# Attention and feed-forward layer with an emitted order: halved first load, two memsets on GpSimd, new weights for the last blocks, another tail

## The chip, the cores and the metric

The kernel runs on one core of one Trainium2 chip. The metric is the time of one execution in device microseconds; a run is timed several times and its median counts. A core has five engines that take their own instructions in order and wait for each other by semaphores: PE (TensorE, matrix multiplications into PSUM), ACT (ScalarE, activations such as exp), DVE (VectorE), POOL (GpSimd) and SP (SyncE, which here only issues DMAs). DMAs are also issued from ACT's and POOL's queues.

## The reference

A layer on x of 2048 rows and 448 columns in bf16. The rows are normalised; attention with 16 heads of 28 columns and a feed-forward part of 1792 columns both start from the normalised rows, and the result is x plus the attention's output times a gate.

```python
def _A_ref(x, wqkv, wo):                      # x: normalised rows, H = 16, Dh = 28
    q, k, v = (x @ wqkv).reshape(B, S, 3, H, Dh).transpose(2, 0, 3, 1, 4)
    scores = jnp.einsum("bhqd,bhkd->bhqk", q, k) * Dh ** -0.5
    p = _softmax(scores, axis=-1)
    o = jnp.einsum("bhqk,bhkd->bhqd", p, v)
    return o.transpose(0, 2, 1, 3).reshape(B, S, D) @ wo
def _B_ref(x, w1, b1, w2, b2):
    return _gelu(x @ w1 + b1) @ w2 + b2
xn = _layernorm(x)
s = _A_ref(xn, A_wqkv, A_wo)
g = _silu(_B_ref(xn, B_w1, B_b1, B_w2, B_b2))
return x + s * g
```

## The kernel before

**Tiling.** The 2048 query rows are four chunks C of 512 (each four row tiles t of 128), the 16 heads four groups G of four heads; head columns are padded from 28 to 32, so that four heads fill 128 partitions. A block is one group with one chunk, 16 blocks in all, the last one (group 3, chunk 3) cut along its queries into pieces of 256, 128 and 128. A score tile is 128 keys by 512 queries of one head, 1024 in all; PE writes it into one of the eight PSUM banks (tile `ring`, matmuls of L1701). ACT takes two banks at once (128x1024) or three (128x1536) through exp (L1755) into bf16 tiles. A part of the score tiles, the late ones, goes another way: DVE reads the bank (L2035) and makes the exponential with integer arithmetic (L2108). PV matmuls (L2283) multiply the probabilities with v; v has an extra column, so that the softmax's denominators come out in the same bank. DVE forms the reciprocal (L2333), multiplies (L2338), and PE applies Wo (the matmul helper, L129). The feed-forward part and the projections fill PE between the scores.

**Order.** No order is written out by hand. The Python program holds every step as a task of an engine, with what it reads and writes and an assumed duration, and `run` (L422) picks the next task of each engine by weights; the instructions are emitted in the order that it picks. The table `BP` has one row of weights for each block, and `NQ` the number of late groups of four score tiles that a block is to have. Weights change the order of instructions only. A task with priority `HOT` goes first, and while `K.hot` holds a time for an engine, no other task that would still run at that time is started on it.

**Start.** `loads` (L936) issues the loads: SP takes row tile 0 and row tile 1 of the first chunk of x, ACT's queue tiles 2 and 3 (L945), two slices of the q and k weights (L952) and the first tile of chunk 1 (L955). DVE computes the statistics of tiles 0, 1 (L1017), ACT those of tile 3 (L1040, L1046); L1053 and L1055 make the reciprocal standard deviation, L1072 (DVE) and L1076 (POOL) the normalised rows, which PE transposes. The value weights `wv` are 128x4x452 with four padding columns, and rows 64 to 127 of the fourth part are padding as well; `late_pads` sets the padding to zero on DVE (L860 to L862), `vpads` sets the extra columns of v on POOL (L925, L926).

**Tail.** The last piece of the last block is 128 queries. `p_den` (L2186) copies what is there of the denominators with DVE (L2195), spreads it with a selector matmul into a bank `K.den`, and adds the last score tiles' sums with matmuls of ones (`t_ones`, L2228). `p_epi4` copies the piece's PV bank to `E_sb` with ACT (L2312), `p_norm4` takes the reciprocal of the bank and multiplies. `p_out` and `p_last` apply Wo to the row tile (c, t), and `t_oev` (L2392) brings the result to memory: by default DVE multiplies the bank with the gate (L2404); where `PATH` names the tile and no exps are left, ACT copies the bank (L2400) and DVE multiplies the copy (L2402). For chunk 3 and half of chunk 2, DVE then adds x (L2410) and SP issues the output DMA (L2414); for the others, a DMA of POOL adds to x in memory. L1672 on DVE makes the last gate, that of tile (3, 3).

Of the kernel before, what the change touches and what calls it, by code (L numbers as in the profile page):

```python
# [7 lines left out]
ACTF = mybir.ActivationFunctionType  # L8
ALU = mybir.AluOpType
# [5 lines left out]
D = 448  # L15
# [3 lines left out]
G = 4  # L19
C = 4  # L20
# [31 lines left out]
)  # L52
NQ = (14, 4, 4, 4, 7, 14, 7, 16, 8, 15, 5, 9, 6, 9, 12, 8)
# [51 lines left out]
EA = 1  # L105
# [4 lines left out]
PATH = {(1, 2): 'D', (1, 3): 'D', (2, 0): 'D', (2, 1): 'D', (2, 2): 'D', (2, 3): 'D', (3, 2): 'D', (3, 3): 'D'}  # L110
XADD = ()
# [37 lines left out]
class _Kernel:  # L149
# [127 lines left out]

    def dma(self, E, fn, dsem, reads=(), writes=(), land=None):
# [140 lines left out]
    def run(self):  # L419
        idle = 0  # L420
        while True:
            self.settle()  # L422
            if self.next_m >= MTOT and all(p[3].prio >= 90 if isinstance(p[3], _Task) else p[3][0] == "bank" and self.lq_end and not self.lq for p in self.procs):
                return
# [276 lines left out]
    def schedule(self):  # L701
# [48 lines left out]
        K.n_mg = 0  # L750
        K.blk = 0
# [81 lines left out]
    def constants(self):  # L833
# [22 lines left out]
        def late_pads():  # L856
            yield ("until", lambda: K.b_xnT[0][1].tw is not None)

            def f(eng):
                eng.memset(K.wv[64:128, 3, :], 0.0)  # L860
# [62 lines left out]
        def vpads():  # L923
            yield ("until", lambda: K.b_wsq[0].tw is not None)
            yield _Task(POOL, lambda eng: eng.memset(K.vaug[:, :, :, DH:DH + 1], 2.0), K.b_xn[0], [K.b_vpad0], 1.2, 0.05, VPP)  # L925
            yield _Task(POOL, lambda eng: eng.memset(K.vaug[:, :, :, DH + 1:32], 0.0), [K.b_vpad0], [K.b_vpad], 1.2, 0.05, VPP)  # L926
# [9 lines left out]
    def loads(self):  # L936
# [6 lines left out]
        ld(K.x_sb[:, 0, 0, :], xr[0][:, 0, :], K.s_x0t, [K.b_x0t], 3.2)  # L943
# [1242 lines left out]
    def p_den(self, q, ms):  # L2186
# [9 lines left out]
        K.den = yield ("bank", lambda: K.ready([K.b_E[0]]), 1)  # L2196
        den, td = K.den
        yield _Task(PE, lambda eng: _mm(eng, den[:, 0:128], K.selb[:, :], Ea, True, False), [K.b_E[0], K.b_selb], [td], 0.1, 0.12, 1)
# [19 lines left out]
    def t_ones(self, p):  # L2218
        K = self
        den, td = K.den  # L2220
        fl, rd = [], []
        for m in p:
            ap, tk = K.p_slot(m)
            _, j, pc, _, _ = K.pieces(m)
            rd.append(tk)
            for i, (t, q0, nq, col) in enumerate(pc):
                def f(eng, j=j, q0=q0, nq=nq, col=col, ap=ap, z=(m == MTOT - 1 and i == len(pc) - 1)):
                    return eng.matmul(den[32 * j:32 * j + 32, q0 - 384:q0 - 384 + nq], K.one32[:, :],  # L2228
                                      ap[:, col:col + nq] if len(ap.shape) == 2 else ap[:, col // 128:(col + nq) // 128, :], tile_position=(0, 32 * j), start=False,
                                      stop=z, skip_group_check=True)  # L2230
                fl.append(f)
# [6 lines left out]
        return _Task(PE, fall, rd + [K.b_one32], [td], 0.0155 * len(fl), 0.17, HOT, mode="col")  # L2238
# [67 lines left out]
    def p_epi4(self, s, bank):  # L2306
# [4 lines left out]
        if s == 2 and EA:  # L2311
            yield _Task(ACT, lambda eng: eng.activation(K.E_sb[:, 1, sl], bank[0][:, sl], ACTF.Copy), [bank[1]],  # L2312
                        [K.b_E4[t] for t in ts] + [K.b_E[1]], 0.3, 0.0, 0)
        else:
            yield _Task(DVE, lambda eng: eng.tensor_copy(K.E_sb[:, 1, sl], bank[0][:, sl]), [bank[1]],
                        [K.b_E4[t] for t in ts] + [K.b_E[1]], 0.16 + 0.13 * len(ts), 0.0, 0)
# [5 lines left out]
    def p_norm4(self, t):  # L2322
# [3 lines left out]
        if t == 3:  # L2326
            bank, tok = K.den
        else:
            bank, tok = yield ("bank", lambda: K.g_done[C - 1] and K.ready([tE]), 3)
            yield _Task(PE, lambda eng: _mm(eng, bank[:, 0:128], K.selb[:, :], E, True, True),  # L2330
                        [tE, K.b_selb], [tok], 0.1, 0.12, 3)
        R = K.rf[:, t % 2, :]
        yield _Task(DVE, lambda eng: eng.reciprocal(R, bank[:, 0:128]), [tok], [K.b_rf[t % 2]], 0.96, 0.0, HOT if t == 3 else 1)  # L2333
        if t == 3:
            K.hot = {DVE: K.tE[DVE]}
# [3 lines left out]
                    [K.b_on4[t]], 0.3, 0.0, HOT if t == 3 else 1)  # L2339
        if t == 3:  # L2340
            K.hot = {PE: K.b_on4[3].tw + SEM}
            K.hot[DVE] = K.hot[PE] + 0.43
        K.on4[t] = True

# [47 lines left out]
    def t_oev(self, ps, tok, c, t):  # L2392
# [5 lines left out]
        way = PATH.get((c, t)) if K.exp_u == len(K.units) - 1 and K.next_m >= MTOT else None  # L2398
        if way:
# [8 lines left out]
        if own:  # L2408
# [29 lines left out]
    def p_last(self, t):  # L2438
# [8 lines left out]
        if t == 3:  # L2447
            K.hot = {DVE: tok.tw + SEM}
# [53 lines left out]
```

## Time and profile before

| | us |
|---|---|
| three runs | 414.64, 414.19, 414.06 |
| median | 414.19 |
| profiled execution | 414.75 |
| its span | 412.2 |
| outside the span | 2.56 |

| engine | busy us | share of the span | instructions |
|---|---|---|---|
| PE | 394.2 | 96% | 6146 |
| ACT | 401.4 | 97% | 411 |
| DVE | 345.1 | 84% | 599 |
| POOL | 194.4 | 47% | 218 |

The granted TensorE clock was 1.0 for the whole execution. The span runs from the first to the last event that the profiler saw. Rows of the timeline give the start, the length, the engine, the line, the operation, output and inputs with their shapes, and a count where like neighbours are drawn together; in square brackets stands the idle time before and what ended it. Rows of groups give the count, then busy time and the mean in ns, then idle time before. Rows of the chain give start, length and the work that the end hung on.

### The profile page before, as it was taken

What the parts mean: (1) busy time and instruction counts of PE and PEld (TensorE: products, weight loads), DVE (VectorE), ACT (ScalarE), POOL (GpSimd) and SP (SyncE); (2) the same over time, 40 slices, a digit from 0 to 9 for tenths busy, and PEclk for the clock granted to TensorE, in tenths of its full rate; (3) what the DMA queues carried; (4) which work ended last, traced back from release to release, by engine and by line L of the source; (5) the groups of instructions that cost most, each with busy time, mean ns of one, the idle gap of its engine ahead of it and who ended that gap; (6) DMA issues with size and microseconds to landing.
All of it is one profiled execution on the core that took longest, in us unless ns stands there. A gap on an engine that the chain in (4) does not pass through costs nothing.

```text
span 412.2 us, 14656 instructions
## 1 busy us (share of the span) xinstructions
PE 394.2 (96%) x6146; PEld 143.4 (35%) x6146; DVE 345.1 (84%) x599; ACT 401.4 (97%) x411; POOL 194.4 (47%) x218
## 2 busy tenths in 40 slices
PE   6999999999999999999989999999999999999995
PEld 4443233333322233232224453332333223333453
DVE  8958798896679888989898127999998999899986
ACT  6999999999999999999999999999999999999995
POOL 7594666659983473155633411155156014553041
PEclk9999999999999999999999999999999999999999
DMA  8801110101001010100430100220000103200073
GB/s 251 293 2 42 4 31 2 28 7 27 21 3 30 2 28 7 33 3 1 110 97 14 28 3 7 53 54 13 20 26 7 29 6 58 72 3 27 24 134 102
DMA packets 18784, 17.54 MB, mean 43 GB/s; under 512 B 8942, under 2 KB 15422, under 8 KB 18687
## 3 DMA queue, kind: packets, MB, share of 16 engines
q1 hardware_dynamic: 16878, 13.67, 11.2%
q0 software_dynamic: 1008, 2.49, 3.6%
q8 instruction: 48, 0.79, 0.8%
q10 hardware_dynamic: 832, 0.46, 0.4%
q14 instruction: 18, 0.14, 0.1%
HBM read 12.54 MB, written 2.88 MB: 37 GB/s over the span
## 4 chain that ended last, share of the span: by engine, by line
PE 66%; ACT 18%; issue 7%; DVE 6%; POOL 1%; DMA 1%; DVEq 0%; ACTq 0%; POOLq 0%
PE ring L129 31%; PE ring L1701 18%; PE ring L2283 15%; ACT P L1755 10%; ACT h L1755 7%; DVE st L1017 1%; ACT xnT L1755 1%; PE ring L1514 1%; DVE x_sb L2035 1%; DMA x_sb<-in_A_x_dram 1%; PE ring L1123 1%; DVE h L2035 0%; PE ring L1090 0%; POOL h L1076 0%; DVE vaug L1476 0%
## 5 line engine op out<-in xcount | busy, mean ns | idle before, releaser
L1755 ACT ACTIVATE P<-ring 128x1024 bf16<-128x1024 f32 (+1 forms) x235 | 248.7, 1164 | 1.4 <-PE ring L2283 0.3
L1701 PE MATMUL ring<-qT,kT 32*128 32x512 bf16 (+2 forms) x1132 | 131.4, 359 | 5.6 <-ACT P L1755 1.9
L1755 ACT ACTIVATE h<-ring 128x1024 bf16<-128x1024 f32 (+1 forms) x79 | 85.6, 1175 | 0.4 <-PE ring L2283 0.3
L1701 PEld LDWEIGHTS ring<-qT,kT 32*128 32x128 bf16 x1132 | 36.4, 91 | 120.5 <-ACT P L1755 60.4
L2035 DVE TENSOR_SCALAR vaug<-ring 128x512 uint16<-128x512 f32 x88 | 58.6, 685 | 6.6 <-PE ring L1701 4.6
L129 PE MATMUL ring<-xnT,w 128*32 128x512 bf16 x864 | 57.6, 381 | 0.4 <-DVE w L2035 0.2
L129 PE MATMUL ring<-w,h 128*32 128x448 bf16 x896 | 55.5, 355 | 0.2 <-DVE x_sb L2035 0.2
L2283 PE MATMUL ring<-P,vaug 128*32 128x512 bf16 (+2 forms) x599 | 53.9, 352 | 0.1
L2378 POOL TENSOR_TENSOR qT<-x_sb,E_sb 128x512 bf16<-128x512 f32 x15 | 17.7, 1182 | 67.0 <-PE ring L2283 29.0
L2367 POOL TENSOR_TENSOR rc<-rs,mone 128x16 f32<-128x16 bf16 x11 | 32.7, 2975 | 29.4 <-DMA rs<-E_sb 27.8
L1755 ACT ACTIVATE xnT<-ring 128x1024 bf16<-128x1024 f32 (+1 forms) x40 | 44.0, 1126 | 0.0
L2035 DVE TENSOR_SCALAR w<-ring 128x512 uint16<-128x512 f32 x52 | 34.7, 686 | 2.7 <-PE ring L1701 2.1
L129 PEld LDWEIGHTS ring<-xnT,w 128*32 128x32 bf16 x864 | 20.5, 96 | 26.1 <-issue 6.3
L129 PEld LDWEIGHTS ring<-w,h 128*32 128x32 bf16 x896 | 17.9, 95 | 22.8 <-issue 14.0
L2035 DVE TENSOR_SCALAR h<-ring 128x512 uint16<-128x512 f32 x32 | 21.3, 685 | 3.8 <-PE ring L1701 3.6
L2283 PE MATMUL ring<-h,vaug 128*32 128x512 bf16 (+1 forms) x209 | 23.9, 379 | 0.5 <-ACT P L1755 0.4
L1416 DVE CAST qT<-ring 128x512 bf16<-128x512 f32 x15 | 10.3, 689 | 15.3 <-PE ring L129 15.0
L2283 PEld LDWEIGHTS ring<-P,vaug 128*32 128x32 bf16 x599 | 16.0, 95 | 14.4 <-issue 7.0
L1528 DVE CAST h<-ring 128x512 bf16<-128x512 f32 x24 | 16.4, 688 | 5.0 <-PE ring L129 4.9
L2035 DVE TENSOR_SCALAR x_sb<-ring 128x512 uint16<-128x512 f32 x28 | 18.5, 683 | 2.5 <-PE ring L1701 1.6
L1422 POOL TENSOR_TENSOR qsq<-qT 128x512 bf16<-128x512 bf16 x12 | 12.5, 1040 | 15.6 <-DVE qT L1416 15.6
L129 PE MATMUL ring<-xnT,wk 128*32 128x512 bf16 x232 | 17.9, 383 | 0.0
(245 smaller groups left out, 639.8 us busy)
## 6 DMA issues: line engine op xcount, KB each, us to landing
x_sb<-recs SPq DMA_DIRECT2D x60, 64.0 KB, 2.0
w<-in_B_w_dram SPq DMA_DIRECT2D x1, 1568.0 KB, 7.5
w<-in_B_w_dram SPq DMA_DIRECT2D x1, 1344.0 KB, 7.9
x_sb<-in_A_x_dram SPq DMA_DIRECT2D x2, 448.0 KB, 5.9
out_dram<-in_A_x_dram SPq DMA_DIRECT2D x2, 448.0 KB, 9.2
out_dram<-h POOLq DMA_DIRECT2D x4, 224.0 KB, 5.9
out_dram<-h SPq DMA_DIRECT2D x8, 112.0 KB, 2.0
xnT<-wq POOLq DMA_DIRECT2D x1, 512.0 KB, 5.0
```

What stands on the lines that cost most here:

```text
L129: ins = eng.matmul(out[q:q + 32, :], w[:, q:q + 32], x, tile_position=(0, q), start=start, stop=stop, skip_group_check=True)
L1017: yield _Task(DVE, lambda eng, i=i, t=t: eng.bn_stats(K.st6[:, i, :], K.x_sb[:, c, t, :]), [K.b_x1t if i == 4 else K.b_x[c] if c else K.b_ ...
L1123: return eng.matmul(bank, w[sl, 3, g * 128:(g + 1) * 128], K.xnT[sl, 3, c * 512:(c + 1) * 512], tile_position=pos, start=False, stop=True, ...
L1416: yield _Task(DVE, lambda eng: eng.tensor_copy(qb, bank), [tok], [qr], 0.7, 0.0, dp)
L1422: yield _Task(POOL, lambda eng: eng.tensor_tensor(qs, qb, qb, ALU.mult), [qr], [tq], 1.1, 0.05, 2, port=True)
L1528: yield _Task(DVE, lambda eng: eng.tensor_copy(dst, bank), [tok], wr, 0.69, 0.0, 2)
L1701: return eng.matmul(dst, K.kT[32 * j:32 * j + 32, g, t * 128:(t + 1) * 128], K.qT[32 * j:32 * j + 32, g, c * 512 + q0:c * 512 + q0 + nq], ...
L1755: return eng.activation(reg[:, i0:i0 + n, :], src, ACTF.Exp, scale=SM_SCALE)
L2035: yield _Task(DVE, lambda eng: eng.tensor_scalar(K.part(u, k).bitcast(dt.uint16), K.like(u, bank), SM_SCALE * LOG2E * 128.0, (127.0 - EXP_ ...
L2283: return eng.matmul(acc[32 * j:32 * j + 32, q0:q0 + nq], w, ap[:, col:col + nq] if len(ap.shape) == 2 else ap[:, col // 128:(col + nq) // ...
L2367: yield _Task(POOL, lambda eng: eng.tensor_tensor(K.rc[:, :], K.rs[:, :], K.mone[:, 0:1].to_broadcast([128, 16]), ALU.pow), [K.b_srs, K.b_ ...
L2378: yield _Task(POOL, lambda eng: eng.tensor_tensor(dst, K.rb, E, ALU.mult), [K.b_rb, tE], [K.b_onT[g][c]], 1.15, 0.05, 1, port=True)
```

## The change

There are four parts.

1. In the table of weights, the rows of blocks 12 to 15 get other values (two of the copies behind them are dropped), and `NQ` asks block 13 for 8 late groups instead of 9.
2. The first row tile of x comes in two halves: rows 0 to 63 from SP, rows 64 to 127 from ACT's queue, ahead of that queue's other loads; both count up the same semaphore.
3. Two of the three memsets of the value weights' padding go from DVE to POOL, ahead of the memsets of v's extra columns and behind the squares of a weight (L1161), each with a wait for the one before; the small one stays on DVE.
4. In the tail, `p_norm3` takes the place of the copy to `E_sb` and of `p_norm4` for the last piece: DVE multiplies the PV bank with the reciprocal directly. The selector matmul into the bank of the denominators gets priority. `PATH` loses (1, 3), (3, 2) and (3, 3) and gains (3, 1). `XADD` gives the addition of x for tile (2, 0) to POOL. For tile (2, 3), listed in `PADD`, PE writes x into a bank by a matmul with the identity and adds the gated result by another, ACT copies the bank, and SP issues the DMA from there. `raw` emits an instruction in place, without the planner's choice.

The diff, cut:

```diff
-NQ = (14, 4, 4, 4, 7, 14, 7, 16, 8, 15, 5, 9, 6, 9, 12, 8)
+NQ = (14, 4, 4, 4, 7, 14, 7, 16, 8, 15, 5, 9, 6, 8, 12, 8)
...
-EA = 1
+HX = 0.1
+PADD = ((2, 3),)
...
-PATH = {(1, 2): 'D', (1, 3): 'D', (2, 0): 'D', (2, 1): 'D', (2, 2): 'D', (2, 3): 'D', (3, 2): 'D', (3, 3): 'D'}
-XADD = ()
+PATH = {(1, 2): 'D', (2, 0): 'D', (2, 1): 'D', (2, 2): 'D', (2, 3): 'D', (3, 1): 'D'}
+XADD = ((2, 0),)
...
         def late_pads():
             yield ("until", lambda: K.b_xnT[0][1].tw is not None)
-            def f(eng):
-                eng.memset(K.wv[64:128, 3, :], 0.0)
-                eng.memset(K.wv[0:64, 3, D:WS], 0.0)
-                return eng.memset(K.wv[:, 0:3, D:WS], 0.0)
-            yield _Task(DVE, f, [], [K.b_wvpad], 0.4, 0.05, 1)
+            yield _Task(DVE, lambda eng: eng.memset(K.wv[0:64, 3, D:WS], 0.0), [], [K.b_wvpad], 0.4, 0.05, 1)
...
         def vpads():
             yield ("until", lambda: K.b_wsq[0].tw is not None)
+            K.wait(POOL, K.b_wsq[0].w)
+            K.raw(POOL, lambda eng: eng.memset(K.wv[64:128, 3, :], 0.0), [K.b_wvpad])
+            K.wait(POOL, K.b_wvpad.w)
+            K.raw(POOL, lambda eng: eng.memset(K.wv[:, 0:3, D:WS], 0.0), [K.b_wvpad])
+            K.wait(POOL, K.b_wvpad.w)
...
-        ld(K.x_sb[:, 0, 0, :], xr[0][:, 0, :], K.s_x0t, [K.b_x0t], 3.2)
+        ld(K.x_sb[0:64, 0, 0, :], xr[0][0:64, 0, :], K.s_x0t, [], 3.2)
+        K.dma(ACT, lambda eng: eng.dma_start(K.x_sb[64:128, 0, 0, :], xr[0][64:128, 0, :]), K.s_x0t, writes=[K.b_x0t], land=3.2)
...
-        if s == 2 and EA:
-            yield _Task(ACT, lambda eng: eng.activation(K.E_sb[:, 1, sl], bank[0][:, sl], ACTF.Copy), [bank[1]], ...)
+        if s == 2:
+            K.E_done = NBLK - 1 + s
+            yield from K.p_norm3(*bank)
+            K.banks.append(bank)
+            return
...
+    def p_norm3(self, acc, ta):
+        (d0, td), = K.den
+        R = K.rf[:, 1, :]
+        yield _Task(DVE, lambda eng: eng.reciprocal(R, d0[:, 0:128]), [td], [K.b_rf[1]], 0.96, 0.0, HOT)
+        K.hot = {DVE: max(K.tE[DVE], ta.tw + SEM)}
+        K.banks += K.den
+        dst = K.qT[:, g, c * 512 + 384:c * 512 + 512]
+        yield _Task(DVE, lambda eng: eng.tensor_tensor(dst, acc[:, 384:512], R, ALU.mult), [ta, K.b_rf[1], K.b_qT[g][c]], [K.b_on4[3]], 0.3, 0.0, HOT)
+        K.hot = {PE: K.b_on4[3].tw + SEM}
+        K.hot[DVE] = K.hot[PE] + 0.43 + HX
+        K.on4[3] = True
...
+        if own and (c, t) in PADD and way:
+            bank, tk = yield ("bank", lambda: True, 1)
+            yield _Task(PE, lambda eng: _mm(eng, bank[:, 0:D], K.ident[:, :], xx, True, False), [K.b_x2[c], K.b_id], [tk], 0.19, 0.17, 1)
         if way:
             yield _Task(ACT, lambda eng: eng.activation(o, ps, ACTF.Copy), [tok], [wr], 0.48, 0.0, 1)
...
+        if own and (c, t) in PADD and way:
+            f = lambda eng: _mm(eng, bank[:, 0:D], K.ident[:, :], o, False, True)
+            yield _Task(PE, f, [K.b_id, wr], [tk], 0.19, 0.17, HOT)
+            yield _Task(ACT, lambda eng: eng.activation(o, bank[:, 0:D], ACTF.Copy), [tk], [wr], 0.48, 0.0, 1)
+            K.outs.append(K.dma(SP, lambda eng: eng.dma_start(ov[:, t, :], o), ...))
```

More of the change, by code (lines that the diff above doesn't have):

```diff
@@ L422, in run @@
             self.settle()
-            if self.next_m >= MTOT and all(p[3].prio >= 90 if isinstance(p[3], _Task) else p[3][0] == "bank" and self.lq_end and not self.lq for p in self.procs):
+            if self.next_m >= MTOT and not self.px and all(p[3].prio >= 90 if isinstance(p[3], _Task) else p[3][0] == "bank" and self.lq_end and not self.lq for p in self.procs):
                 return
@@ L2195, in p_den @@
         yield _Task(DVE, lambda eng: eng.tensor_copy(Ea, acc[:, sl]), [tok], [K.b_E[0]], 0.29, 0.0, 0)
-        K.den = yield ("bank", lambda: K.ready([K.b_E[0]]), 1)
-        den, td = K.den
-        yield _Task(PE, lambda eng: _mm(eng, den[:, 0:128], K.selb[:, :], Ea, True, False), [K.b_E[0], K.b_selb], [td], 0.1, 0.12, 1)
+        K.den = []
+        K.hot = {PE: K.b_E[0].tw + SEM}
+        for c0, c1 in ((0, 128),):
+            x = yield ("bank", lambda: True, HOT)
+            K.den.append(x)
+            yield _Task(PE, lambda eng, d=x[0], c0=c0, c1=c1: _mm(eng, d[:, c0:c1], K.selb[:, :], Ea[:, c0:c1], True, False), [K.b_E[0], K.b_selb], [x[1]], 0.08, 0.12, HOT)
+        K.hot = {}
+        td = K.den[0][1]
         for n0, n1, one in DEN:
@@ L2226, in t_ones, with f @@
             for i, (t, q0, nq, col) in enumerate(pc):
[L2227 to L2230, printed above, removed]
+                def f(eng, j=j, col=col, ap=ap, z=(m == MTOT - 1 and i == len(pc) - 1)):
+                    src = ap[:, col:col + 128] if len(ap.shape) == 2 else ap[:, col // 128, :]
+                    for (d, _), c0, c1 in zip(K.den, cut, cut[1:]):
+                        ins = eng.matmul(d[32 * j:32 * j + 32, c0:c1], K.one32[:, :], src[:, c0:c1], tile_position=(0, 32 * j), start=False,
+                                         stop=z, skip_group_check=True)
+                    return ins
                 fl.append(f)
@@ L2310, in p_epi4 @@
         yield ("until", lambda: K.on_done[NBLK - 3])
-        if s == 2 and EA:
[L2312 to L2316, printed above, removed]
+        if s == 2:
[3 more added lines that the diff above has]
+            return
+        yield _Task(DVE, lambda eng: eng.tensor_copy(K.E_sb[:, 1, sl], bank[0][:, sl]), [bank[1]],
+                    [K.b_E4[t] for t in ts] + [K.b_E[1]], 0.16 + 0.13 * len(ts), 0.0, 0)
         K.E_done = NBLK - 1 + s
@@ L2325, in p_norm4 @@
         E, tE = K.E_sb[:, 1, 128 * t:128 * (t + 1)], K.b_E4[t]
[L2326 to L2331, printed above, removed]
+        bank, tok = yield ("bank", lambda: K.g_done[C - 1] and K.ready([tE]), 3)
+        yield _Task(PE, lambda eng: _mm(eng, bank[:, 0:128], K.selb[:, :], E, True, True),
+                    [tE, K.b_selb], [tok], 0.1, 0.12, 3)
         R = K.rf[:, t % 2, :]
-        yield _Task(DVE, lambda eng: eng.reciprocal(R, bank[:, 0:128]), [tok], [K.b_rf[t % 2]], 0.96, 0.0, HOT if t == 3 else 1)
-        if t == 3:
-            K.hot = {DVE: K.tE[DVE]}
+        yield _Task(DVE, lambda eng: eng.reciprocal(R, bank[:, 0:128]), [tok], [K.b_rf[t % 2]], 0.96, 0.0, 1)
         K.banks.append((bank, tok))
@@ L2447, in p_last @@
         if t == 3:
-            K.hot = {DVE: tok.tw + SEM}
+            K.hot = {DVE: tok.tw + SEM + HX}
         yield from K.t_oev(ps, tok, c, t)
```

27 lines of the change are left out of this document (20 added, 7 removed), and 10 rows, old and new, of the table BP.

## The prediction, made before the changed kernel ran

> **What bounds the kernel now.** I read the page's busy times and its chain first, then the timeline of ACT, then ACT's groups in the stretch that the change reorders.
>
> ```profile
> span 412.2 us, 14656 instructions
> PE 394.2 (96%) x6146; PEld 143.4 (35%) x6146; DVE 345.1 (84%) x599; ACT 401.4 (97%) x411; POOL 194.4 (47%) x218
> PE 66%; ACT 18%; issue 7%; DVE 6%; POOL 1%; DMA 1%; DVEq 0%; ACTq 0%; POOLq 0%
> ```
>
> ACT is busy 97% of the span and PE 96%; the chain that ended last gives PE 66% and ACT 18%. So the two run neck and neck: ACT takes one exp after another, and PE has to lay the next scores down in time. The timeline of ACT tells which of them is late (start, length, line, operation, count):
>
> ```profile
> 12.67 10.32 ACT L1755 ACTIVATE P<-ring 128x1024 bf16<-128x1024 f32 x11
> ...
> 372.02 1.13 ACT L1755 ACTIVATE xnT<-ring 128x1024 bf16<-128x1024 f32 x1
> 372.92 1.56 ACT L1755 ACTIVATE P<-ring 128x1536 bf16<-128x1536 f32 x1
> 374.25 1.15 ACT L1755 ACTIVATE xnT<-ring 128x1024 bf16<-128x1024 f32 x1
> ...
> 385.20 1.07 ACT L1755 ACTIVATE xnT<-ring 128x1024 bf16<-128x1024 f32 x1
> 386.40 4.41 ACT L1755 ACTIVATE P<-ring 128x1536 bf16<-128x1536 f32 x4
> ...
> 397.03 4.78 ACT L1755 ACTIVATE P<-ring 128x1024 bf16<-128x1024 f32 x5
> 401.55 1.18 ACT L1755 ACTIVATE xnT<-ring 128x1024 bf16<-128x1024 f32 x1
> 402.86 1.94 ACT L1755 ACTIVATE P<-ring 128x1024 bf16<-128x1024 f32 x2
> 404.69 1.03 ACT L1755 ACTIVATE xnT<-ring 128x1024 bf16<-128x1024 f32 x1
> ```
>
> The distance from one start to the next is the price of an exp with nothing in the way: (401.55 − 397.03)/5 = 0.904 us for 1024 columns, 374.25 − 372.92 = 1.33 us for 1536. A longer distance is a stall: 386.40 − 385.20 = 1.20, so 0.30 too much; 402.86 − 401.55 = 1.31, so 0.41 too much. From the first exp at 12.67 to the end of the last at 404.69 + 1.03 = 405.72 the time is exps plus such stalls. Three things are therefore left for the change: when the first exps start, the stalls in the stretch that it reorders, and the tail after 405.72.
>
> **Part 1, the start.** Rows of the timelines of DVE, ACT, PE and POOL, and POOL's group for a plain memset:
>
> ```profile
> 3.53 1.36 DVE L1017 BATCH_NORM_STATS2 st<-x_sb 128x6 f32<-128x448 bf16 x2 [0.20 <-DMA x_sb<-in_A_x_dram]
> ...
> 5.82 0.73 DVE L1072 TENSOR_SCALAR h<-x_sb,mv,rstd 128x448 bf16<-128x448 bf16 x2
> ...
> 10.38 0.25 DVE L860 MEMSET wv<- 64x226 uint32 x1
> 10.66 0.47 DVE L1261 TENSOR_SCALAR qT<-ring,colK 128x256 bf16<-128x256 f32 x1
> ```
>
> ```profile
> 0.75 0.39 ACTq L945 DMA_DIRECT2D x_sb<-in_A_x_dram  x1
> 3.76 0.58 ACT L1040 ACTIVATE P<-x_sb 128x448 bf16<-128x448 bf16 x1 [1.75 <-DMA x_sb<-in_A_x_dram]
> ```
>
> ```profile
> 11.08 0.97 PE L129 MATMUL ring<-wv,xnT 128*32 128x112 bf16 x64
> 13.88 0.38 PE L1090 MATMUL ring<-ident,h 128*128 128x128 bf16 x4 [0.51 <-DVE st L1017]
> ```
>
> ```profile
> 8.30 1.23 POOL L925 MEMSET vaug<- 128x256 bf16 x1 [0.59 <-DVE h L1072]
> ...
> 12.87 0.87 POOL L1076 TENSOR_SCALAR h<-x_sb,nm,rstd 128x448 bf16<-128x448 bf16 x1 [0.30 <-ACT rstd L1055]
> ```
>
> ```profile
> L1913 POOL MEMSET qpad<- 128x512 bf16 x1 | 0.5, 515 | 0.0
> ```
>
> *The two halves.* DVE stood 0.20 us before its first statistics, waiting for the first x tile. That is the most the halves can bring: after it DVE's own memsets bind. The other way they can cost: ACT's first load, issued at 0.75, was there when L1040 began at 3.76, later than the 3.53 at which the x tile from SP served DVE; if the half on ACT's queue lands like that load, statistics start at 3.76, +0.23. Half the rows should not take as long as that load, so I take −0.10, bounds −0.20 and +0.23. What is queued behind the new issue on ACT: the remaining loads go one issue (0.39) later, so L1040 would run from at most 4.15 to 4.73. DVE's own statistics last to 3.53 + 1.36 = 4.89, which covers it; without that cover it would be 0.39.
>
> *The memsets.* From DVE goes L860 (10.38 to L1261's start at 10.66: 0.28); the 64x2 one that stays is L861's. DVE's q tiles (L1261) come earlier by up to 0.28 plus what the halves bring. But PE's v block (11.08, 0.97 long) and the first scores stand behind work fed by x, so PE moves only by the halves. On POOL come two memsets: 64x452 at no more than L1913's rate, about 0.46, and the 128x12 one, by the same slope near nothing, with its fixed part about 0.1. POOL stood 0.59 before L925; 0.56 plus two waits on its own semaphores fill that hole and push L925 by about 0.05 (0.6 if L1161 had ended later). POOL's xn tile L1076 at 12.87 decides when the transposes at 13.88 and the scores of the third exp come; it waits 0.30 for rstd, and that hides 0.05. Taken: −0.05, bounds −0.20 and +0.10.
>
> Sum for the start: **−0.15**, bounds −0.40 and +0.30.
>
> The Trainium skill ("DMA: Bandwidth & Descriptors", Rules for kernel authors) speaks against the halves: two transfers to disjoint partition halves serialize on the same DMA engines, so one of 128 partitions should be used. The 3.53 row cannot tell, as no tile is split before; by the rule the halves would bring 0 and the start −0.05 (rival 1). The skill's "SBUF — State Buffer" (Who interferes with whom) has DVE's tensor_scalar and GpSimd block each other for whole instructions; the two L1072 at 5.82 took 0.73 for both while POOL was at work, so I add nothing for the new memsets there; by that rule the start would be up to 0.46 worse.
>
> **Part 2, the last blocks.** PE's order is the same for its first 5213 instructions of 6148; after that (about 364 us) blocks 13 to 15 are reordered. The number of exps does not change: still as many of 1024 and of 1536 columns. ACT's groups from 372.3 to 404.6, shapes apart (the count stands after x):
>
> ```profile
> L1755 ACT ACTIVATE P<-ring 128x1024 bf16<-128x1024 f32 x17 | 17.0, 1087 | 0.2
> L1755 ACT ACTIVATE xnT<-ring 128x1024 bf16<-128x1024 f32 x9 | 10.0, 1110 | 0.0
> L1755 ACT ACTIVATE P<-ring 128x1536 bf16<-128x1536 f32 x6 | 9.2, 1533 | 0.1
> ```
>
> From the start at 372.02 to the one at 404.69, 32.67 us, lie 26 exps of 1024 (23.50) and 6 of 1536 (7.98): 31.48. So **1.19 us of stall is all that reordering can win here**; more than a third is the one of 0.41. What causes it, from the chain (start, length, work of PE):
>
> ```profile
> 400.95 0.94 PE ring L129 x16
> 401.89 0.61 PE ring L2283 x32
> 402.50 0.69 PE ring L1701 x16
> ```
>
> Sixteen matmuls of Wo and 32 of PV, 1.55 us, lay between two groups of scores, where ACT had an exp of 0.904 to chew. In the changed order I summed the same way, with these prices, the PE work between score groups. The single steps that preceded a stall (1.62 ahead of 386.40, then 1.95, then 1.87 over two exps) become 1.46 and 1.41 for one exp, and 1.68, 1.52, 1.62 and 2.06 for two. About 0.7 us of the stall should go; the last step grows (32 PV, 24 Wo and 4 selector matmuls ahead of the last scores) and gives back 0.1 to 0.2, smaller ones another 0.15 to 0.25. Taken: **−0.30**, bounds −1.1 (nearly stall-free) and +0.5 (a new order as poor as the worst such stretch I summed elsewhere in the trace, with some 0.35 more stall, and the last step at its upper price).
>
> **Part 3, the tail.** T is the end of the last exp, 405.72.
>
> ```profile
> 404.10 0.62 DVE L2404 TENSOR_TENSOR h<-ring,h 128x448 bf16<-128x448 f32 x1
> ...
> 406.24 0.96 DVE L2333 RECIPROCAL w<-ring 128x128 f32<-128x128 f32 x1 [0.88 <-PE ring L2228]
> 407.30 0.29 DVE L2338 TENSOR_TENSOR qT<-E_sb,w 128x128 bf16<-128x128 bf16 x1
> 407.51 0.38 DVE L1672 TENSOR_TENSOR h<-h,w 128x448 bf16<-128x448 bf16 x1
> ```
>
> ```profile
> 407.65 0.37 PE L129 MATMUL ring<-wo,qT 128*32 128x448 bf16 x4
> 407.68 0.98 ACT L2400 ACTIVATE h<-ring 128x448 bf16<-128x448 f32 x2 [0.21 <-PE ring L129]
> ...
> 408.54 0.69 DVE L2402 TENSOR_TENSOR h<-h 128x448 bf16<-128x448 bf16 x2
> 408.65 1.71 SPq L2414 DMA_DIRECT2D out_dram<-h  x3
> 409.14 0.69 DVE L2410 TENSOR_TENSOR h<-h 128x448 bf16<-128x448 bf16 x2
> ```
>
> Before: reciprocal at T + 0.52, multiply T + 1.58, Wo's last four at T + 1.93, then ACT's copy (to 408.66), DVE's multiply and add (to 409.83 = T + 4.11), then the last output DMA: SP's three issues end at 408.65 + 1.71 = 410.36, and less one issue of 0.39 (as ACT's at 0.75) the last begins at T + 4.25. After: the last exp is one of 1536 columns, so 16 ones matmuls instead of 8 follow it: reciprocal at T + 0.58, its multiply straight from PSUM at T + 1.64 to 1.93 (ACT's copy to E_sb was not late, so its loss saves nothing), Wo to T + 2.35. ACT's copy, half of 0.98 plus the hand-over, and DVE's L2402 leave the path of (3,3); in their place stands one L2404 from PSUM, 0.62 as at 404.10: T + 2.45 to 3.07; the add to T + 3.49. The other late tile, (2,3), gets PE's identity matmuls (0.37 as the row at 407.65) at T + 2.58, ACT's copy 2.98 to 3.52, its DMA issue at T + 3.55. That issue stands ahead of the last one on SP's queue; with 0.39 for it the last begins at T + 3.94, not 3.52. **−0.31**; bounds −0.45 (SP's hold shorter) and +0.10 (reciprocal held by the DVE's L2404 and add of (3,2), which just fit ahead of it).
>
> **Sum.** −0.15 − 0.30 − 0.31 = −0.76. The profiled execution took 414.75 us (412.2 of span and 2.56 around it), so 414.0 there. The three runs have a median of 414.19, the profiled one being the slowest of four; on the median the forecast is 414.19 − 0.76 = 413.43, **413.4**. Its own range, from the start and the last blocks at half or double: −0.3 to −1.2, 413.0 to 413.9.
>
> **Rivals.**
> *1, nothing at the start and nothing in the blocks (413.9).* Both halves land together with what one transfer did, and the reordered blocks move their stalls instead of losing them; −0.31 remains. For it: the stalls before are only 0.3% of the span. Against: the 0.41 one has a plain cause that the new order lightens. Chance 0.12.
> *2, faster (412.4).* The last blocks come out nearly stall-free (−1.1), the start gives its whole −0.40, the tail −0.3: −1.8. For it: ACT ran such stretches already, 397.03 to 401.55 without a stall. Against: PE is 96% busy, so what leaves one gap enters another. Chance 0.24.
> *3, slower (415.3).* The last exp's 12 score matmuls use the bank that DVE's L2404 of tile (3,1) frees, and DVE reaches that only after a copy (0.29 as the multiply), a reciprocal (0.96), a multiply (0.29) and L2404 itself (0.62): 2.16 us in order. ACT then has one or two exps in hand, 0.90 to 1.81, and the scores add about 0.33: a stall of 2.16 + 0.33 − 1.81 = 0.7 to 2.16 + 0.33 − 0.90 = 1.6. It decides from the point where that reciprocal starts less than 1.9 us before PE wants the bank; I count 0.25 us of slack. At 1.6 with the start nearly as before (−0.2) and the tail's −0.31 it is +1.1, 415.3; at 0.7 the whole is about even. For it: DVE takes its queue in order and is 84% busy. Against: the slack is worked out, not guessed, and the order before met no such stall between 402.86 and 404.69. Chance 0.18, of which 0.13 slower.
>
> **How the numbers follow.** Forecast 0.46, rivals 0.12, 0.24 and 0.18. About 0.2%, 0.83 us, is what a measurement of this kernel can tell from no change, and the forecast lies just inside it: I give 0.25 of its 0.46 to faster, 0.21 to same. Faster 0.25 + 0.24 = 0.49, same 0.21 + 0.12 + 0.05 = 0.38, slower 0.13. The range goes from rival 2's middle, 412.4, to 414.9, which takes in rival 3's small end and leaves out some 0.1 on each side.
>
> **What would show it.** First statistics at 3.35 to 3.45 and the first exps 0.1 to 0.2 earlier; over 0.2 later at 3.76 if ACT's half is late. From 372 to the last exp's start, starts further apart than 0.904 or 1.33 add to about 0.9, the largest just before the last exp; over 1.9 there means rival 3, under 0.3 rival 2. The last output issue at about 3.9 after the last exp's end. It is wrong if stalls appear before 364 us, where the order is the same, or if the tail grows.

## The result, and the profile after

The changed kernel takes 416.25 us (median of 8 runs, 415.58 to 417.91), the one before 414.37 (8 runs, 414.06 to 414.88): a ratio of 1.0049, 95% interval 1.0034 to 1.0064. The forecast was 413.4, at most 414.9. By the medians the change costs 1.9 us. Of its eight runs, three (417.45 to 417.91) had a mean granted TensorE clock of 0.996, and the other five (415.58 to 416.64, median 415.85) one of 0.998 to 1.0. The profiled span grew from 412.2 to 413.9.

The page after, its span, busy times and chain:

```profile
span 413.9 us, 14687 instructions
PE 394.9 (95%) x6157; PEld 143.3 (35%) x6157; DVE 346.0 (84%) x595; ACT 400.6 (97%) x409; POOL 195.9 (47%) x221
PE 62%; ACT 20%; issue 8%; DVE 6%; POOL 2%; DMA 1%; ACTq 0%; DVEq 0%; POOLq 0%
```

Busy times hardly moved (PE 0.7 more, ACT 0.8 less), so most of the 1.7 us of span are waiting. Most of this waiting is there before the first exp. The timeline of ACT and its queue after (the line numbers are those of the changed file: L952 is the new half, L954 the load of tiles 2 and 3, L961 the weight slices, L964 the first tile of chunk 1):

```profile
0.77 0.58 ACTq L952 DMA_DIRECT2D x_sb<-in_A_x_dram  x1
1.39 0.82 ACTq L954 DMA_DIRECT2D x_sb<-in_A_x_dram  x1
2.24 0.97 ACTq L961 DMA_DIRECT2D h<-in_A_wqkv_dram  x2
3.24 0.69 ACTq L964 DMA_DIRECT2D x_sb<-in_A_x_dram  x1
...
7.66 0.39 ACT L1158 ACTIVATE wq<-h 128x224 bf16<-128x224 bf16 x1 [1.30 <-DMA h<-in_A_wqkv_dram]
...
13.91 2.95 ACT L1764 ACTIVATE P<-ring 128x1024 bf16<-128x1024 f32 x3
```

The same of before, two rows that the prediction did not show:

```profile
1.17 0.97 ACTq L952 DMA_DIRECT2D h<-in_A_wqkv_dram  x2
2.17 0.49 ACTq L955 DMA_DIRECT2D x_sb<-in_A_x_dram  x1
```

The first exp starts at 13.91 instead of 12.67, 1.24 later. The last load of ACT's queue is issued at 3.24 instead of 2.17: the new half took 0.58 and made the load behind it take 0.82 instead of 0.39. What that does to DVE (timeline after):

```profile
3.36 1.36 DVE L1026 BATCH_NORM_STATS2 st<-x_sb 128x6 f32<-128x448 bf16 x2
...
8.08 0.63 DVE L1026 BATCH_NORM_STATS2 st<-x_sb 128x6 f32<-128x448 bf16 x1 [1.51 <-DMA x_sb<-in_A_x_dram]
8.62 0.99 DVE L1081 TENSOR_SCALAR h<-x_sb,mv,rstd 128x448 bf16<-128x448 bf16 x2
```

The first statistics do start 0.17 earlier, at 3.36, as forecast; but f4 and f2 below, with the tile in one load, start them at 3.36 and 3.38 too, so the runs do not show that the halves did it. The statistics of chunk 1's first tile wait 1.51 for their data and start at 8.08, and before they started at 6.64 without a wait for a load:

```profile
6.64 0.62 DVE L1017 BATCH_NORM_STATS2 st<-x_sb 128x6 f32<-128x448 bf16 x1
```

The chain that ended last runs through that very load:

```profile
3.24 4.81 DMA x_sb<-in_A_x_dram
8.05 0.02 issue
8.08 0.45 DVE st L1026
```

The loads' issue-to-landing times, ACT's queue, after and then before (median where there are two):

```profile
h<-in_A_wqkv_dram ACTq DMA_DIRECT2D x2, 56.0 KB, 3.8
x_sb<-in_A_x_dram ACTq DMA_DIRECT2D x1, 112.0 KB, 4.8
```

```profile
h<-in_A_wqkv_dram ACTq DMA_DIRECT2D x2, 56.0 KB, 3.0
x_sb<-in_A_x_dram ACTq DMA_DIRECT2D x1, 112.0 KB, 3.6
```

So the tile of chunk 1 is issued 1.07 later and takes another 1.2 to land: about 2.3 later in all, against a cover of about 0.85 that it had before. The later of the two weight slices takes 4.9 to land instead of 3.0, and ACT waits for the weights until 7.66. What else was in flight shows on SP's queue, its 336-KB load of the rest of chunk 1, after and then before:

```profile
3.18 0.59 SPq L948 DMA_DIRECT2D x_sb<-in_A_x_dram  x1
```

```profile
2.91 0.58 SPq L940 DMA_DIRECT2D x_sb<-in_A_x_dram  x1
```

Before, ACT's last load was issued 0.74 ahead of that big one (2.17 against 2.91); after, 0.06 behind it (3.24 against 3.18).

By the twelfth exp the delay is 1.63 instead of 1.24, and it stays at 1.63 up to 378 us. In the last blocks, ACT's timeline after:

```profile
396.01 1.10 ACT L1764 ACTIVATE P<-ring 128x1024 bf16<-128x1024 f32 x1
397.36 1.02 ACT L1764 ACTIVATE xnT<-ring 128x1024 bf16<-128x1024 f32 x1 [0.24 <-PE ring L1710]
398.28 5.65 ACT L1764 ACTIVATE P<-ring 128x1024 bf16<-128x1024 f32 x6
404.31 1.03 ACT L1764 ACTIVATE xnT<-ring 128x1024 bf16<-128x1024 f32 x1 [0.38 <-PE ring L1710]
```

By the prices of 0.904 and 1.33, the 32 exps that start from 373.64 to the last one's start at 406.13 (27 of 1024 columns, 5 of 1536) contain 1.43 of stall, where the 32 of before had 1.19. The largest are 0.44 at 397.36 and 0.49 at 404.31. The second hangs on this piece of the chain:

```profile
401.98 0.55 DVE h L2433
402.52 0.04 issue
402.57 1.38 PE ring L128 x28
403.94 0.33 PE ring L1710 x8
```

A multiply of DVE from PSUM, at the end of a run of reciprocals and multiplies that the chain follows from 397.53, lets PE start 28 Wo matmuls at 402.57, and only behind these come the scores of the exp at 404.31. The tail, DVE and SP:

```profile
408.20 0.96 DVE L2359 RECIPROCAL w<-ring 128x128 f32<-128x128 f32 x1
...
410.08 0.62 DVE L2433 TENSOR_TENSOR h<-ring,h 128x448 bf16<-128x448 f32 x1
410.73 0.39 DVE L2447 TENSOR_TENSOR h<-h 128x448 bf16<-128x448 bf16 x1
```

```profile
411.21 0.33 SPq L2443 DMA_DIRECT2D out_dram<-h  x1
411.58 0.43 SPq L2451 DMA_DIRECT2D out_dram<-h  x1
```

With the last exp's end at 407.59 as T, the last output issue begins at T + 3.99, 0.22 less than in the kernel before (409.93, T + 4.21).

### The profile page after: what moved, and what is told of

The parts are those of the page before. It is cut to its first block, busy times and chain, and to the rows that moved or that the text cites. A ratio compares the mean times of both kernels' runs of the same rounds, so it can differ in the third digit from the quotient of the medians.

```text
span 413.9 us, 14687 instructions
## 1 busy us (share of the span) xinstructions
PE 394.9 (95%) x6157; PEld 143.3 (35%) x6157; DVE 346.0 (84%) x595; ACT 400.6 (97%) x409; POOL 195.9 (47%) x221
## 3 DMA queue, kind: packets, MB, share of 16 engines
q0 software_dynamic: 1008, 2.49, 3.6%
HBM read 12.54 MB, written 2.88 MB: 37 GB/s over the span
## 4 chain that ended last, share of the span: by engine, by line
PE 62%; ACT 20%; issue 8%; DVE 6%; POOL 2%; DMA 1%; ACTq 0%; DVEq 0%; POOLq 0%
PE ring L128 30%; PE ring L1710 16%; PE ring L2299 14%; ACT P L1764 11%; ACT h L1764 7%; ACT xnT L1764 2%; DMA x_sb<-in_A_x_dram 1%; PE ring L1523 1%; DVE x_sb L2044 1%; DVE st L1026 1%; POOL h L1085 1%; PE ring L1132 1%; DVE h L2044 0%; PE ring L1099 0%; DVE w L2347 0%
## 5 line engine op out<-in xcount | busy, mean ns | idle before, releaser
L1710 PEld LDWEIGHTS ring<-qT,kT 32*128 32x128 bf16 x1131 | 35.5, 91 | 120.3 <-ACT P L1764 59.5
L2044 DVE TENSOR_SCALAR vaug<-ring 128x512 uint16<-128x512 f32 x92 | 61.1, 684 | 5.9 <-PE ring L1710 3.8
L1764 ACT ACTIVATE xnT<-ring 128x1024 bf16<-128x1024 f32 (+1 forms) x39 | 43.0, 1130 | 0.6 <-PE ring L1710 0.6
L2299 PE MATMUL ring<-h,vaug 128*32 128x512 bf16 x201 | 23.4, 383 | 0.5 <-ACT P L1764 0.4
L2044 DVE TENSOR_SCALAR h<-ring 128x512 uint16<-128x512 f32 x28 | 18.8, 686 | 3.8 <-PE ring L1710 3.6
```

What stands on the lines that cost most here:

```text
L1710: return eng.matmul(dst, K.kT[32 * j:32 * j + 32, g, t * 128:(t + 1) * 128], K.qT[32 * j:32 * j + 32, g, c * 512 + q0:c * 512 + q0 + nq], ...
L1764: return eng.activation(reg[:, i0:i0 + n, :], src, ACTF.Exp, scale=SM_SCALE)
L2044: yield _Task(DVE, lambda eng: eng.tensor_scalar(K.part(u, k).bitcast(dt.uint16), K.like(u, bank), SM_SCALE * LOG2E * 128.0, (127.0 - EXP_ ...
L2299: return eng.matmul(acc[32 * j:32 * j + 32, q0:q0 + nq], w, ap[:, col:col + nq] if len(ap.shape) == 2 else ap[:, col // 128:(col + nq) // ...
```

## The experiments

Kernels that differ only at the start run the same instructions in the same order on PE, ACT and DVE (the moved memsets and loads apart), so each part can be had alone. The times below are medians; "before" ran on the same chip within each group of four. The first exp's start is from each kernel's profile (12.67 in the profile of before; g2, g3 and g4, which have its start, show 12.76 to 12.88, so 0.2 there tells nothing).

| kernel | us | before | ratio, 95% interval | first exp |
|---|---|---|---|---|
| f1 halves alone | 417.40 | 414.51 | 1.0057 [1.0035, 1.0079] | 14.46 |
| f2 memsets alone | 414.74 | 414.51 | 1.0000 [0.9986, 1.0015] | 12.76 |
| f3 both halves from SP | 416.91 | 414.51 | 1.0050 [1.0033, 1.0067] | 15.07 |
| f4 extra 1-KB load on ACT | 416.83 | 414.51 | 1.0038 [1.0021, 1.0056] | 16.09 |
| g1 halves, SP's big load held | 414.71 | 414.67 | 1.0000 [0.9986, 1.0014] | 12.91 |
| g2 change without its start | 414.61 | 414.67 | 1.0000 [0.9989, 1.0010] | 12.88 |
| g3 new weights alone | 415.08 | 414.67 | 1.0018 [1.0006, 1.0030] | 12.76 |
| g4 new tail alone | 414.56 | 414.67 | 0.9992 [0.9979, 1.0005] | 12.82 |
| h1 change, SP's big load held | 415.33 | 414.96 | 1.0013 [1.0000, 1.0027] | 12.63 |
| h2 change, one slice moved to SP | 415.00 | 414.96 | 1.0004 [0.9989, 1.0019] | 13.15 |
| h3 change, first tile in one load | 415.07 | 414.96 | 1.0011 [0.9996, 1.0025] | 12.67 |
| h4 before, SP's big load earlier | 415.19 | 414.96 | 1.0012 [1.0000, 1.0024] | 13.52 |

**f1, the halves alone.**

```diff
-        ld(K.x_sb[:, 0, 0, :], xr[0][:, 0, :], K.s_x0t, [K.b_x0t], 3.2)
+        ld(K.x_sb[0:64, 0, 0, :], xr[0][0:64, 0, :], K.s_x0t, [], 3.2)
+        K.dma(ACT, lambda eng: eng.dma_start(K.x_sb[64:128, 0, 0, :], xr[0][64:128, 0, :]), K.s_x0t, writes=[K.b_x0t], land=3.2)
```

> The kernel before with one part of the change alone: the first x tile in two halves, one from SP and one from ACT's queue. Theory A (the new issue at the head of ACT's queue makes that queue's other loads late): the first x tile lands at about 3.2 instead of 3.5, tiles 2 and 3 at about 4.6 instead of 3.7, the first tile of chunk 1 at about 8 instead of 5.8; the first exp starts at about 13.9 instead of 12.67, and the time rises by 1.4 to 1.9 us, so nearly all of the measured +1.9. Theory B (the two memsets on GpSimd hold the start up): no change or a gain, 414.0 to 414.5, first exp at 12.5 to 12.7. Theory C (cutting the tile in two is what costs, wherever the halves are issued): as A here.

Measured: +2.9 us by the medians, +0.57% by the comparison (1.5 to 3.3 us, where A had 1.4 to 1.9), first exp at 14.46. The halves alone cost what the whole change costs, and B falls. The timeline of DVE has the same wait, longer:

```profile
8.72 0.63 DVE L1018 BATCH_NORM_STATS2 st<-x_sb 128x6 f32<-128x448 bf16 x1 [2.13 <-DMA x_sb<-in_A_x_dram]
```

**f2, the memsets alone** (the two moved as in the change's diff).

> The kernel before with the two memsets of the value weights' padding moved to GpSimd alone. Theory A: within 0.2 us of before (414.2 to 414.5), first exp at 12.5 to 12.7, the memsets inside GpSimd's hole of 0.59 us ahead of the memsets of v. Theory B: GpSimd's chain comes 0.5 us or more later, the first exps at 13.2 or later and the time at 415 or more.

Measured: no difference beyond the interval of ±0.15%. In its profile the exps fall 0.48 behind by the twelfth, so a few tenths are there; see h3.

**f3, both halves from SP.**

```diff
-        K.dma(ACT, lambda eng: eng.dma_start(K.x_sb[64:128, 0, 0, :], xr[0][64:128, 0, :]), K.s_x0t, writes=[K.b_x0t], land=3.2)
+        ld(K.x_sb[64:128, 0, 0, :], xr[0][64:128, 0, :], K.s_x0t, [K.b_x0t], 3.2)
```

> The kernel before with the first x tile in two halves, both from SP; ACT's queue is left as it was. Theory A: ACT's loads land as before (the first tile of chunk 1 at about 5.8 to 6.1), SP's later loads come 0.4 to 0.6 later; the first exp within 0.4 us of 12.67, the time between 414.2 and 414.9. Theory C: the first exp at about 13.9 and 415.8 to 416.3, as with halves from two queues.

A's number is missed: +0.50%. ACT's loads are as before, but now the first tile itself is late. DVE's first statistics:

```profile
4.91 1.36 DVE L1018 BATCH_NORM_STATS2 st<-x_sb 128x6 f32<-128x448 bf16 x2 [1.58 <-DMA x_sb<-in_A_x_dram]
```

The second half is issued behind the first, at 1.39, and takes 3.5 to land (chain):

```profile
1.39 3.50 DMA x_sb<-in_A_x_dram
```

So DVE starts at 4.91 instead of 3.53, and A is too narrow: it is not ACT's queue that is special. On either queue, what is pushed back is late by more than its issue. SP's 336-KB load is issued only at 3.81 here and not beside the half, so theory D, which the next runs test, does not cover this case. Why the first exp comes 2.40 later when the first statistics come 1.38 later was not followed.

**f4, an extra load of 1 KB on ACT's queue**, with the whole first tile from SP.

```diff
+        K.dma(ACT, lambda eng: eng.dma_start(K.P[0:64, NP - 1, 0:8], xr[0][64:128, 0, 0:8]), K.s_x0b, writes=[], land=3.2)
```

> The kernel before with the whole first tile from SP, and one extra load at the head of ACT's queue that moves only 64 rows of 16 bytes into a spare place that nobody reads. Theory A: the queue's other loads are pushed back as in the change, with nothing gained by an earlier tile: the first exp at 13.5 to 14.1, the time at 415.6 to 416.4. Theory C, or contention by the bytes of the half: within 0.3 us of before.

Measured: +0.38%, and in its profile chunk 1's first tile comes latest of all:

```profile
0.77 0.55 ACTq L944 DMA_DIRECT2D P<-in_A_x_dram  x1
```

```profile
9.04 0.63 DVE L1018 BATCH_NORM_STATS2 st<-x_sb 128x6 f32<-128x448 bf16 x1 [2.42 <-DMA x_sb<-in_A_x_dram]
```

C falls: no tile is cut here, and 1 KB is enough. What costs is one more issue at the head of the queue. But an issue of 0.55 does not explain 2.4: ACT's last load is issued at 2.97 instead of 2.17 and lands some 6.0 after that instead of 3.6. In f1, f4 and the changed kernel its issue falls just beside that of SP's 336-KB load. Theory D says that this company is the price, and g1 and h4 test it from both sides.

The first exp at 16.09, later than A's 13.5 to 14.1, is not the work of the loads alone. In this profile the granted TensorE clock was 0.50 from 12 to 14 us, where it was 1.0 in the kernel before; why it fell is not shown (the window's length, busy time of PE, PEld, DVE, ACT and POOL, then the clock, the DMA share and GB/s):

```profile
12.00:14.00 2.00, 2.00 (x11) 1.45 (x10) 1.64 (x6) 0.95 (x4) 1.94 (x6) 0.50 1.08 309
```

**g1, the halves with SP's big load held back** by two issues of 1 KB.

```diff
+        K.dma(SP, lambda eng: eng.dma_start(K.P[0:64, NP - 1, 448:456], xr[0][64:128, 0, 0:8]), K.s_x[1], writes=[], land=3.2)
+        K.dma(SP, lambda eng: eng.dma_start(K.P[0:64, NP - 1, 456:464], xr[0][64:128, 0, 0:8]), K.s_x[1], writes=[], land=3.2)
         ld(K.x_sb[:, 1, 1:4, :], xr[1][:, 1:4, :], K.s_x[1], [K.b_x[1]], 6.5)
```

> The kernel with the two halves alone, and on SP two extra loads of 1 KB each (64 rows of 16 bytes into a place that nobody reads) right ahead of its 336-KB load of chunk 1's other tiles, so that this load is issued some 1 us later. Theory A, refined to D (what ACT's queue was pushed back by costs most because its last loads then run beside SP's 336-KB load): the last weight slice of ACT's queue lands at about 5.5 to 6 instead of 8, the first tile of chunk 1 at 6 to 7 instead of 8.7; the first exps at 12.8 to 13.8 and the time at least 0.8 us under that of the halves alone (417.4), if the later 336-KB load (about 8.5 to 9) does not take it back. Rival E (each load is late by the issues ahead of it alone, whatever runs beside it): those two land as with the halves alone, and the time is that or up to 1 us more.

Measured: the loss of the halves is gone, 414.71 against 414.67, with more loads, and those of ACT's queue issued later than before. ACT's last load is issued at 3.24 just as in the changed kernel, SP's big one now at 4.46, and the landing time of the former (DMA view) falls from 4.8 to 3.0:

```profile
4.46 0.58 SPq L940 DMA_DIRECT2D x_sb<-in_A_x_dram  x1
```

```profile
x_sb<-in_A_x_dram ACTq DMA_DIRECT2D x1, 112.0 KB, 3.0
```

```profile
6.47 0.62 DVE L1020 BATCH_NORM_STATS2 st<-x_sb 128x6 f32<-128x448 bf16 x1
```

DVE's statistics of chunk 1's tile are back at 6.47, without a wait. E falls. It also shows the most that the halves are worth when nothing is pushed into company: nothing that these runs can tell.

**g2, the change without its start; g3, the new weights alone; g4, the new tail alone** (each the corresponding part of the change's diff).

> The changed kernel with the start of before: one load of the first x tile, memsets on DVE. What is left is the new order of the last blocks and the new tail. Theory A: the first exp at 12.67, the steady part as before, the last exp's start about 0.2 us earlier than before but 0.43 us longer, the tail 0.2 to 0.3 us shorter: 414.0 to 414.6, within 0.1% of before. Rival F (the last blocks hold most of the loss): 415.5 or more.

> The kernel before with the new weights for blocks 12 to 15 and the new number of late groups alone; its tail is that of before. As in the changed kernel some 1.2 to 1.6 us of stall stand between 372 and the last exp: the end of the last exp 0 to 0.4 us later than before and the time 414.3 to 414.9. If the reordering was good and only its match with the new tail bad: 413.5 to 414.1.

> The kernel before with the new tail alone (no copy of the last piece's bank, the direct multiply, x added by PE for one tile, the new paths); weights, late groups and start are those of before. The prediction's tail term of -0.31 says 413.9 to 414.3, the last output's issue at about 3.9 us after the end of the last exp; as measured in the changed kernel, 4.0 us. If the tail saves nothing on its own: 414.4 to 414.7.

Measured: g2 equals before within 0.11%, so the loss is in the start, and F falls. The new weights alone lose 0.18%. The new tail alone wins 0.08%, which its interval does not tell from nothing, though its last output is issued 4.02 after the last exp's end instead of 4.21. In g2 the same two stalls as in the changed kernel, 0.44 and 0.50, are there, 1.43 in all.

**h1, the change with SP's big load held** (g1's two lines), **h2, with one weight slice on SP**, and **h3, with the first tile in one load** (memsets, weights and tail as in the change).

```diff
-        lw(0, 4 * DH, K.s_w["wqk"], K.b_stg, 6.1, (ACT, ACT, SP, SP))
+        lw(0, 4 * DH, K.s_w["wqk"], K.b_stg, 6.1, (ACT, SP, SP, SP))
```

> The changed kernel in full, with the two extra loads of 1 KB on SP ahead of its 336-KB load, nothing else. Theory D (the whole loss is that ACT's pushed-back loads run beside SP's 336-KB load): the last weight slice of ACT's queue and the first tile of chunk 1 land at about 6.0 and 6.2 as in the halves with the same hold, the first exp at 12.7 to 13.1, and the time falls from 416.3 to 414.3 to 414.8, no faster than before. Rival G (the memsets on GpSimd, which now lie beside DVE's work, cost by themselves in this start): 415.0 to 415.6.

> The changed kernel with one weight slice's load moved from ACT's queue to SP's, so that ACT's queue has as many loads as before and SP's 336-KB load is issued one place later; no extra load. Theory D: the first tile of chunk 1 is again issued ahead of the 336-KB load and lands at 5.7 to 6.5; the first exp at 12.7 to 13.5 and the time at 414.3 to 415.0, unless a weight slice becomes the late one (SP's last at 6.5 to 7.5). Rival E (only the issues ahead of each load count): SP's slices and its 336-KB load later by half a us, 414.8 to 415.5.

> The changed kernel with the first x tile in one load from SP again; memsets on GpSimd, last blocks and tail as in the change. Theory D: the loads land as before, the time 414.3 to 414.9, equal to before within 0.15%. Rival G: 415.0 or more.

Measured: all three are within 0.15% of before, against +0.49% for the change: holding the big load, having one load fewer in front, or not cutting the tile, each takes the loss away, though their intervals reach up to 0.27%. As absolute times h1's 415.33 and h3's 415.07 lie in G's ranges; but the kernel before, 414.19 to 414.67 in the earlier groups, took 414.96 in this one. Against that the three medians are 0.04 to 0.37 higher, which is D's side with room for a few tenths of G. In h2 the first exp comes at 13.15, because SP's last weight slice is now the late one, as its expectation allowed for. The profiles of h1 and h3 show the rest: the first exp starts with that of before (12.63 and 12.67), the twelfth about 0.37 later in both. In h3, DVE and POOL at the new memset (L929 is the 64x452 one, L933 the first of v's columns):

```profile
7.38 0.99 DVE L1080 TENSOR_SCALAR h<-x_sb,mv,rstd 128x448 bf16<-128x448 bf16 x2
```

```profile
7.75 0.49 POOL L929 MEMSET wv<- 64x452 bf16 x1
8.29 0.12 POOL L931 MEMSET wv<- 128x12 bf16 x1
8.52 1.23 POOL L933 MEMSET vaug<- 128x256 bf16 x1
```

The memsets fill POOL's hole and 0.22 more (8.52 instead of 8.30), and the two tensor_scalars of DVE beside them take 0.99 instead of 0.76. DVE makes that good, as it no longer has the memset of 0.28: it reaches its next tensor_scalar level with before. But POOL is still behind, with its own normalisation of a tile beside that at 11.83 instead of 11.62, and this tensor_scalar and the next take longer, h3 and then before:

```profile
12.11 0.57 DVE L1080 TENSOR_SCALAR h<-x_sb,mv,rstd 128x448 bf16<-128x448 bf16 x1
...
13.13 0.64 DVE L1080 TENSOR_SCALAR h<-x_sb,mv,rstd 128x448 bf16<-128x448 bf16 x1
```

```profile
7.40 0.76 DVE L1072 TENSOR_SCALAR h<-x_sb,mv,rstd 128x448 bf16<-128x448 bf16 x2
...
12.12 0.36 DVE L1072 TENSOR_SCALAR h<-x_sb,mv,rstd 128x448 bf16<-128x448 bf16 x1
...
12.94 0.37 DVE L1072 TENSOR_SCALAR h<-x_sb,mv,rstd 128x448 bf16<-128x448 bf16 x1
```

That G costs a few tenths is what the profiles agree on: between the first exp and the twelfth, all five with the memsets on POOL (the changed kernel, f2, h1, h2, h3) lose 0.37 to 0.40 against before, and f1, g1 to g4 and h4, with the memsets on DVE, at most 0.01. The times alone do not prove it.

**h4, the kernel before with SP's 336-KB load one place earlier**, ahead of SP's last weight slice; ACT's queue untouched.

> The kernel before with SP's 336-KB load of chunk 1's other tiles put one place earlier, ahead of SP's last weight slice; ACT's queue is untouched and has no extra load. Theory D: ACT's last weight slice and the first tile of chunk 1, issued at 1.65 and 2.17 as before, land 0.7 to 2.5 later than the 4.7 and 5.8 of before, since they now run beside the 336-KB load; SP's own last slice lands at about 7; the first exp 0.5 to 2 later and the time 414.9 to 416.5. Rival E: ACT's two land as before; only SP's own slice is late.

Measured: +0.12% [0.00, 0.24], first exp at 13.52. The landing tells D from E: ACT's last load is issued at the same 2.17, now with the big one at 2.10, and takes 4.9 instead of 3.6 (3.5 to 4.1 in all the profiles in which these two issues stand as before).

```profile
2.17 0.49 ACTq L957 DMA_DIRECT2D x_sb<-in_A_x_dram  x1
```

```profile
x_sb<-in_A_x_dram ACTq DMA_DIRECT2D x1, 112.0 KB, 4.9
```

```profile
7.12 0.63 DVE L1018 BATCH_NORM_STATS2 st<-x_sb 128x6 f32<-128x448 bf16 x1 [0.45 <-DMA x_sb<-in_A_x_dram]
```

The same load, issued at the same time from the same place in its queue, is 1.3 later because another queue's big load starts beside it. That shows D's landing by itself, but not its price. The first exp of this run hung on another load, SP's last weight slice, which the edit put behind the big one (chain):

```profile
2.61 4.75 DMA h<-in_A_wqkv_dram
```

And the time, 0 to 1.0 us above before, does not tell D's 0.7 or more (414.9 against 414.2) from nothing. No version beat the kernel before by more than its interval.

## Why the prediction was wrong

**The start was the step that failed**, −0.15 forecast, +1.6 in the profile; of this the halves, −0.10 forecast, were +1.24 at the first exp. The paragraph on the halves did name what is queued behind the new issue, but then priced only the first of these loads, the tiles 2 and 3 that L1040 reads, and priced it by the issue alone, 0.39. That reader started at 4.62, not at most 4.15, but the cover named did hold: L1062, the next that needs ACT, starts at 5.20, as L1053 did at 5.21. The last two loads of the same queue, a weight slice and chunk 1's first tile, were never followed to their readers; their rows at 1.17 and 2.17 stood in the view that was read. The tile's reader started at 6.64 with its data there since about 5.8, and the push came to 2.3: 0.64 until the load behind could be issued (1.39 instead of 0.75), another 0.43 because that issue grew, and 1.2 of company with SP's 336 KB, which no row before could have priced but the order of issues (2.17 ahead of 2.91) could have flagged. The sign named for the start, first statistics at 3.35 to 3.45, came true and was luck: it watched a reader that was not the late one. Rival 1 followed the rule of the Trainium skill that two halves serialize. The runs do not refute it: the halves landed 2.8 and 3.1 us into the span and the whole tile of before at 3.5, but in f4 the whole tile, with only ACT's 224-KB load issued later, landed at 2.8. The harm came from elsewhere. The page of the Trainium skill that bears on it is the same, "DMA: Bandwidth & Descriptors", section "Issuing engines are not separate DMA queues": transfers started by different engines run on the same DMA engines and interleave. h4's 4.9 against 3.6 agrees with it.

**The memsets**, −0.05 forecast, some +0.39 in the profiles: the hole was 0.59 wide as read, but two waits and the memsets took 0.8, so POOL fell 0.22 behind. The pair of tensor_scalars beside them grew by 0.23, and the two after them, beside POOL's late normalisation, by 0.21 and 0.27; the prediction had let POOL's delay hide behind L1076's wait. I had set such growth to nothing from one pair of 0.73 beside another POOL operation. This is read from the rows; no run takes it apart. The Trainium skill's "SBUF — State Buffer" (Who interferes with whom) was nearer here, though not to its letter: by a full block for the memset's whole 0.49, the pair would have taken about 1.25, not 0.99.

**The last blocks**, −0.30 forecast, +0.24 measured (the stalls add to 1.42 or 1.43 in the profiles of g2, h1 and h3 as well), inside the bounds and on the wrong side. The sum of PE work between scores took PE as never waiting. The largest new stall came where PE waited for DVE's run of reciprocals and then had 28 Wo matmuls ahead of the scores: rival 3's mechanism, at an earlier exp than rival 3 named and for 0.5 instead of 0.7 to 1.6. This is read from the chain and was not taken away by an experiment.

**The tail** was right: reciprocal forecast at T + 0.58, found at 0.61; last multiply 2.45 and 2.49; last issue 3.94 and 3.99. Its −0.31 came to −0.22, as the last issue of before stood at T + 4.21 and not at the 4.25 worked out for it. This and the blocks' +0.24 cancel, as g2 shows. The weights and the tail belong together: with the weights alone (g3) the last output is issued 5.14 after the last exp's end, and 0.18% is lost.

So of the sum, one term held, one was off by half a us with the wrong sign, and the start, bounded at +0.30, decided the result. A stall before 364 us was named as a sign of being wrong, and it came. The rival that would have ended at 416 was missing, and so the range, 412.4 to 414.9, was too narrow. Two slips in the sums changed none of this: the start's upper bounds add to +0.33, and the start and the blocks at half, with the tail, give −0.5 and not −0.3.

## What to carry to other kernels

When a DMA is put at the head of a queue, follow every load behind it to its reader, and compare its new issue time with the issues of the other queues: a load that slips from ahead of a big transfer to beside it can pay more than the slip (2.3 us for one of 1.07 here). Where several queues load at once, tune the order of issues across queues, not only within each. If such a loss is found, try to delay the big transfer before giving up the edit: two issues of 1 KB won back the halves' loss here (g1), and the whole change's to within 0.27% (h1).

## What the runs showed of the hardware that was not expected

A load of 64 rows held its queue longer than one of 128 rows: 0.58 for 56 KB and 0.55 for 1 KB, against 0.39 for 112 or 224 KB at the head of a queue, and the 224-KB load behind it took 0.82 (0.59 behind the 1-KB one). A 112-KB load took 3.0 to land with the other queue's 336-KB load held back (g1), 3.6 in the kernel before, and 4.8 to 6.0 when issued beside that load (the changed kernel, h4, f1, f4). Two tensor_scalars of 128x448 beside a memset on GpSimd took 0.99 together instead of 0.76 (h3). Two later ones in h3 ended 0.13 to 0.14 after the tensor_scalar of GpSimd beside them (12.68 after 12.54, 13.77 after 13.64) and took 0.57 and 0.64, not 0.36 and 0.37 as before.
